# Attention with a convolution-gated FFN: w_in in three loads, V shifts by halves, and a new order table with its own buffer counts

One NeuronCore of a Trainium2 chip runs the whole program. The metric is the device time of one execution in microseconds (us); lower is better. The medians quoted are of all runs of a kernel, a few slow ones included (one of four of the kernel before, 230.82 us).

## The reference

Sliding-window attention over 8 batches, 8 heads, 576 positions and 64 features per head (window of 32 to either side), then an FFN whose hidden layer is gated by a depthwise convolution of three taps along the sequence. Condensed:

```python
scores = scale * np.matmul(q, k.transpose(0, 1, 3, 2))
scores = np.where(np.abs(pos[:, None] - pos[None, :]) <= 32, scores, -1e9)
attn = softmax(scores);  x = (attn @ v) -> (8, 576, 512)
h = np.maximum(x @ w_in, 0.0)                   # (8, 576, 1024)
conv_out = sum(conv_w[k] * shifted(h, k) for k in range(3))
gate = 1.0 / (1.0 + np.exp(-conv_out))
return (h * gate) @ w_out                       # (8, 576, 512), float32
```

## The kernel before

The program is a list of operations and a table that fixes everything about their execution. A token such as `286S1` means: operation 286, on engine S, with buffer 1. The letters are P for TensorE, V for VectorE (DVE in the profile), S for ScalarE (ACT), G for GpSimd (POOL), D for a DMA queue and F for filler matmuls on a zero tile. Each engine executes its own tokens strictly in the order of the table, so a token that isn't ready holds up all the later tokens of its engine. Two on-chip memories are named: the program's matmuls write to PSUM, and its loaded, cast and intermediate tiles are in SBUF.

The FFN is cut into 12 chunks of 384 positions, and each chunk into 8 units of 128 hidden features (chunk 1 into 16 half units). A unit is a projection on TensorE (`ph`, into PSUM), a relu into `hT` (in SBUF, bf16), three convolution taps, a tanh, and the gate into `gT`. Six kinds of unit split the taps between TensorE, GpSimd and VectorE (condensed):

```python
TAPS = {   # kind: (taps on TensorE, on GpSimd, on VectorE)
    "3": ((0, 1, 2), (), ()), "2": ((0, 2), (), (1,)), "1": ((0,), (), (1, 2)),
    "q": ((), (0, 2), (1,)), "r": ((), (0,), (1, 2)), "s": ((0,), (1, 2), ()),
}
def emit_times(e_, cp, kk):                # GpSimd: a product, "cp" in the profile
    gpsimd.tensor_scalar(out=in3(cp.ap), in0=taps(kk), scalar1=w_tap(kk), scalar2=0.0, op0=ALU.mult, op1=ALU.add)
def emit_add(e_, cps=cps):                 # GpSimd: the sum of two products
    gpsimd.tensor_tensor(out=in3(cps[0].ap), in0=in3(cps[0].ap), in1=in3(cps[1].ap), op=ALU.add)
def emit_pc(e_, on_pe=on_pe):              # TensorE: matmuls with diagonal weights, into PSUM
    for kk in on_pe: tensor.matmul(pc.ap[:, 0:nc_], diag_w[:, kk, m, :], taps(kk), ...)
def emit_tap(e_, kk, from_):               # VectorE: pc = hT * weight + from_
    vector.scalar_tensor_tensor(
        out=in3(pc.ap), in0=taps(kk), scalar=w_tap(kk), in1=in3(from_.ap), op0=ALU.mult, op1=ALU.add)
def emit_sum(e_, cps=cps):                 # VectorE: pc = pc + cp
    vector.tensor_tensor(out=in3(pc.ap), in0=in3(pc.ap), in1=in3(cps[0].ap), op=ALU.add)
```

`from_`: in the kinds 2 and 1 it is a PSUM bank, which TensorE's taps have filled. In the kinds q and r it is, for the first tap on VectorE, a `cp` buffer in SBUF, which GpSimd has filled; as `hT` is in SBUF too, that tap has two inputs in SBUF. I call it a "tap from cp". The mask multiplication of the attention (`attn * mask`) has two SBUF inputs as well, and the gate has one (`pc` is in PSUM).

V is needed at even and at odd 64-row offsets; `vo` is the shifted copy of `ve`:

```python
def shift_v(b, c0, c1):
    op(f"vo hi {b} {c0} {c1}", lambda e: copy(e, vo[0:64, c0:c1], ve[64:128, c0:c1]), ...)
    op(f"vo lo {b} {c0} {c1}", lambda e: copy(e, vo[64:128, c0:c1], ve[0:64, c0 + 1:c1 + 1]), ...)
```

The softmax here doesn't subtract the row's maximum and nothing guards it: scores larger than these inputs give would overflow.

Of the kernel before, what the change touches and what calls it, by code (L numbers as in the profile page):

```python
# [10 lines left out]
BF16 = mybir.dt.bfloat16  # L11
# [29 lines left out]
class Work:  # L41
# [44 lines left out]
BUFS = {'st': 3, 'qkb': 5, 'qkT': 3, 'attn': 2, 'rec': 4, 'xn': 3, 'hT0': 8, 'hT1': 6, 'hT2': 6, 'cp': 2, 'gT': 4, 'y': 7}  # L86
TURNS = ('eeeee', 'eeede', 'eeeed', 'dedde', 'ddddd', 'ddddd', 'ddddd', 'edddd')
CONV = (
    '33333333',
    '33q3323r23223321',  # L90
    's222r32q',
    '1232s332',
    '22q22q22',
    'q31s2qrq',
    '33212q2s',
    'r2rq312q',
    'qq23q1q2',
    'r3rqrq23',
    '12qrrq1q',
    '2rrr2rrq',  # L100
)
ORDER = """
15D 11D0 12D 1F 17D 2F 13D1 2F 14D 7F 28G 0V 1P0 2F 2V 33V 1F 4G 4F 20G0 21S 2F 16D 5G 1F 22S1 41P120 42P 23S 3G
45P34 44V 1F 43S 1F 46P 8G 2F 48S 47V 1F 9G 1F 30S 2F 49P5600 24G2 25S 54P214 2F 37V 18D 55S 1F 10G 1F 51S 1F 120D2
59P321 60P 52S 26V3 1F 27S 1F 6G 62V 1F 63P60 19D 61S 1F 64P 1F 36V 50S 121D0 1F 7G 65V 2F 130D1 66S 2F 53V 29S 1F
67P2351 1F 57S 56S 1F 35G 131D 72P604 70S 1F 31V 68S 2F 34G 1F 73S 2F 38V 74S 1F 39V 1F 58V 69S 3F 75S 123G 135D 1F
125S 77P10 86P5 124S 71V 95P2 3F 122G 78V0 96V1 1F 87V2 79S 2F 32V 132D2 2F 76V 97S 3F 40G 88V 1F 133D 98P6 89P0
113P3 99V3 107P4 90V0 104P1 100V 80P2 128G 129S 1F 114V1 105V2 1F 81V3 91V 102P5 127S 126G 106V 1F 93P6 82S 108V0
103V 139G4 109V 115S 84P7 94V 111P0 231D0 85S 112V 118P1 156P522 140G0 119V 134D 241P4 158S 157V 285P3 242S00 263P6
286S1 144V 243P7 264S2 149G 287P0 261S 150V 265P1 141G1 305S 262V 307P2 283S 306V 159P54 284V 142G2 308S3 172P360  # L110
161V 329P7 136D 174S 160V 173S 309P0 351P1 330S4 327S 331P2 232D1 352S5 328V 162P4650 233G 234S 353P3 349S 235V 137D
373P7 165S 164S 350V 163S 175P10 374V6 143G 167P526 371S 395P4 176V 236S 985D 170S 166V 375P7 169S 517P1 396S7 145G
372V 473P6 168S 177V 397P2 152G 393S 429P4 415S 171V 178P3501 138D 430S01 238S 239G 518V1 583P4 416V 181S 519P1 240S
237G 474V2 539P0 986D 394V 180S 451P2 482G0 983D2 561P6 179S 148V 495P7 481G1 584S3 188P51 151V 452S4 417P3 483G
496V5 537S 987D 189V2 190S 981D0 538V 146G 453P4 982D 183P271 182V 562S1 984D 471S 197P5 147S 418P 595G0 186S 198V3
484V6 185S 155G 199V 431P1 184S 472V 497P7 153V 421P5 419S0 154V 994V 988D 515S 187V 540S4 206P4 449S 422P 493S
992S3 450V 207V0 494V 516V 209P2 596V3 200P0 208S 191P1 218P6 996G 210V1 201V2 215P7 192V3 211V 202S 193V 542P2
219V1 213P4 216V0 423V1 195P1 217S 989D 204P0 220V 224P5 196V 990S4 425P6 991G0 225V3 543V 226V 1076D1 1017P711 214S
205V 221D 229P5 559S 426P 1077D 230S 993G1 1018V 1001P402 560V 1080D 427S2 1019V 1004P57 1078D0 627P2 1003S 1002V
1079D 605P6 1006S 715P1 997G 628V0 649P0 606S1 1005V 716S2 629P4 608P7 998G 717P2 647S 650V3 671P6 597V 735S 693P1  # L120
648V 1085G2 672S4 652P5 736V 603S 1020P04 609V 694S5 674P6 604V 625S 695P2 1022V 1021S 737P1 759P3 713S 626V 738S7
563P0 675V 760S6 793P4 714V 581S 1082D 995V 691S 1007P7130 582V 1086S3 1000D 692V 740P2 653V 764P0 815P6 741V 1008S
794V02 1010S 816V2 757S 837P7 809G1 1009S 765V 808G0 758V 1012P436 669S 838S5 766V 781P1 1087G4 670V 1014S 1015S
1081D 1013S 1096P270 1011V 779S 782P 1097S 810G 780V 1098V 1099P53 783S3 1083D 1023P6421 1016V 811P0 1100S 999D
840P7 424D 1088G0 812V 1024S 818P1 859P5 1084D 1101V 1026S 813S 420D 1025S 1112P622 1089G 841V 784D 881P3 860S4 428D
814V 1027G 1113S 1735D2 1114V 862P4 882S3 785P5 857S 819V 863V 1028P062 1737D1 1092S 1033P32 858V 1736D 835S 786P
1738D 1034V2 879S 893G1 836V 1029S 1051P7 1035V 1090G 1031S 1042P1 880V 787S4 1060P0 903P3 1091G 1052V1 1030S 1061V0
1043V3 1053V 925P2 1094D 894V4 904S1 1741D 947P5 1062V 926S0 895V 905P6 1044V 948S5 1115P73 1032V 901S 928P0 923S
955G0 1117V 789P2 1116S 1744G1 924V 1036P1 929V 1045P5 1069P3 1063P7 1054P6 1037V2 956G1 790P 1046V1 945S 1064V0
1038V 1065S 1746G2 1055V3 1047V 1070V2 1040P1 1056V 1049P5 791S5 1071V 1067P7 957G 1058P6 1050S 902V 1072D 1755P321  # L130
1068S 946V 973P4 1745G3 1059S 1756V 1041S 1740D 1102P5070 1757V 1747S4 969P6 788D 958V3 1739D 1093V 1171P1 1105S
1103S 1095D 1104S 1193P2 1172V03 967S 1106G 1215P7 1742D 1750S 1194V2 1107P501 968V 1216S1 1832D0 1176P2 1110S
1196P3 1108S 1177V 970P 1109S 1197V 1833Q 1118P7151 1743D 1178V 1749G 1213S 1237P0 1073D 1120S 1111V 1830D2 974P
1121S 1831D 1191S 1748G 1214V 1238S5 792D 1192V 1128P10 1119S 1146P5 975V6 1155P3 1137P0 971S1 1259P2 1122G 1147V1
1129V0 1156V3 1138V2 1148V 1123P746 1139S 1130V 1217P5 1260V4 1125S 1240P1 1157V 1126S 1277P0 1124S 1303P2 1241V
1835D 1235S 1274G1 1325P4 1257S 1127V 1842S0 1281P3 1275G0 1236V 1158P6 1140P7 1304V7 1326S3 1751G 1131P5 1282S6
1258V 1149P4 1752G 1164P2 1150V1 1305P3 1159V0 1165V2 1151S 1834D 1141V3 1276G 1160V 1283P1 1166V 1323S 1132V0 972D
1328P6 1142V 1754G 1301S 977P2 1278V 1302V 1279S 1144P4 1324V 1771P710 1145S 1280V 978P 1836D 1840G1 1772S 1329V
976D 1161D 1133V 1774P34 1345S 1773V 1758P07 1753D 1839G2 979S0 1347P5 1134D 1759S 1346V 980D 1776V 1844S 1841G4
1169P1 1850P262 1838D 1170S 1348P 1760V 1775S 1843G 1851V 1761P0410 1349S3 1852V 1351P7 1762S 1350D 1845G 1763S  # L140
1766P325 1764S 1853P60 1767S 1765V 1866P411 1352P 1769S 1768S 1868V 1854S 1770G 1837D 1777P3521 1867V 1353S2 1355P1
1855V 1778S 1152D 1780S 1782P647 1354D 1779S 1356P 2491D1 1785S 1784S 2492D 1783S 1781V 2489D2 1359P3 1357S4 1786V
1787P01 2490D 1360S00 1805P2 1814P5 1358D 1796P7 1806V2 1381P4 1788V1 1815V3 1807S 1797V0 1847V 1798V 1403P6 1816S
1382V1 1362P1 1846V 1384P3 1404S2 1789V 1447P7 1363V 1412G0 2495D 1385V 1425P2 1379S 1411G1 1448S3 1817P4 1380V
1401S 1413G 1790P5 1450P0 1426S4 1818V0 1791V2 1402V 1823P6 1808P7 2500G3 1428P1 1451V 1469P2 1809V3 1824V1 1467S
1429V 1810S 1799P3 1468V 1825V 1445S 1491P0 1800V3 1414V7 1826D 1470S5 2501S2 1547P6 1446V 1477G0 1801V 1513P2
2498G1 1492V0 1423S 1869P13 1792V 1548S21 1424V 1494P0 1514S1 1793D 1478G1 1569P5 1870V 1871S 2494D 1479G 2499S4
1827D 1516P6 1819V 1535P7 1495V 1820D 1555G1 1517V 1570S4 1591P2 1511S 1480V3 1533S 1613P1 1512V 1556G0 1489S 2493D
1534V 1592S1 1571P4 1802D 2504G 1614V3 1848D 1635P5 1589S 1557G 1490V 1849D 1596P0 1856P6210 1590V 1636S0 1536P
1597V 1628G0 1857S 1558V3 1859S 1858S 2496D 1861P456 2503G 1598V 1567S 1631P1 1811D 1539P2 1862S 1860V 1611S 1629G1  # L150
1568V 1701P4 1864S 1863S 1612V 1630G 1540P 1537S5 1702V5 2502S 1538D 1872P6351 1865V 1541S1 1877P074 2497D 1874S
1709G1 1632V 1657P2 2584D0 1879S 1710G0 1542D 1679P3 1878S 2586D1 1711G 1875S 1882P72 1873S 2587D 1891P0 1900P5
1883V1 1880S 1892V3 1633S 1909P6 1884V 1638P4 1658S4 1881V 1543P7 2585Q 2505G 1893V 1680S2 1910V2 1925P2 1634V 1911S
1665G0 2589D 1901V0 1639V 2507D 1544P 1926S22 1902V 1655S 1876V 1927P0 1545S6 1947P3 1712V1 2506S 1546D 1656V 1918P6
1945S 1691G1 1894P2 1885P5 1948S0 1919V1 1903P7 1946V 1912P4 1721S 1991P3 1895V3 1913V2 1904V0 1896S 1920V 2508D
2593G0 1914V 2035P0 1886V1 1905S 1722V 2509P640 1887V 1921D 1969P2 1992S1 1692V1 2510S 2594G1 2511V 1949P5 1970S5
2013P7 1693V 2036S6 1888D 1666G1 1967S 1727P3 2014V7 1699S 1667G 1968V 2016P6 1700V 2079P4 1922D 2592Q 2043G1 2017V
# [36 lines left out]
def kernel(  # L194
# [67 lines left out]
    diag_w = sb.tile([128, 3, MB, 128], BF16, name="diag_w")  # L262
    ident = sb.tile([128, 128], BF16, name="ident")
    ident24 = sb.tile([3 * MB, 3 * MB], FP32, name="ident24")
    mask = sb.tile([128, 18, 64], BF16, name="mask")
    zero = sb.tile([128, 512], BF16, name="zero")


# [541 lines left out]
```

## Time and profile before

| | |
|---|---|
| median time (4 runs, 227.18 to 230.82) | 227.36 us |
| span of the profiled execution | 225.6 us |
| units of full width: 3 / 2 / q / r / 1 / s | 19 / 25 / 19 / 14 / 7 / 4 |
| filler matmuls | 75 |

The prediction below shows the busy row, the windows and the main groups. First the groups of instructions by form: line, engine, operation, output <- inputs, shapes, count, then busy time, mean duration in ns, and idle time of the engine before them.

```profile
L232 DVE SCALAR_TENSOR_TENSOR pf<-hT,conv_w_sb,cp 128x384 f32<-128x384 bf16 x33 | 20.4, 630 | 0.0
L232 DVE COPY vo<-ve 64x520 bf16<-64x520 bf16 x10 | 4.1, 410 | 0.7 <-ACT ve L232 0.5
```

The first row is the taps from cp: 33 of them, 630 ns each; the second the V shifts on VectorE. Then the wait list (total, times, longest): ScalarE's tanh waits 11.1 us for taps of VectorE.

```profile
ACT pf L232 <- DVE pf L232: 11.1, 18, 1.2
```

And the chain of work that ended last, as shares of the span by engine:

```profile
PE 41%; DVE 18%; ACT 17%; DMA 13%; issue 5%; SPq 3%; POOL 2%; DVEq 0%; ACTq 0%; POOLq 0%
```

### The profile page before, as it was taken

Reading aid. Unit: us, or ns where it says so; the run is one execution under the profiler, and the core shown is the slowest. Engines: PE = TensorE matmul, PEld = TensorE weight load, DVE = VectorE, ACT = ScalarE, POOL = GpSimd, SP = SyncE. Lnnn points to the kernel's source line nnn. Section 1 sums busy time; section 2 is a strip of 40 time slices with the busy share of each in tenths; the row PEclk is TensorE's granted clock in tenths of the full one; section 3 lists DMA queues with packets and bytes.
Section 4 is the critical chain, followed back from the end, with each engine's and each line's share of the span. In section 5 each row is a group of like instructions: output and inputs, shape, how many; then the busy total and the mean of one; then the engine's idle time right before and its main releaser. Section 6 shows DMA issues by size and latency. Waiting matters only on the chain.

```text
span 225.6 us, 7189 instructions
## 1 busy us (share of the span) xinstructions
PE 211.5 (94%) x2720; PEld 122.9 (54%) x2720; DVE 197.3 (87%) x467; ACT 187.5 (83%) x474; POOL 137.7 (61%) x203
## 2 busy tenths in 40 slices
PE   7698899989989999989999998999999999999993
PEld 5366567658555655545555454545655565455541
DVE  6279869899999979797999788989999999899990
ACT  2689899998989889879889989689989999777642
POOL 5978654654376937695368736756386735566640
PEclk9889999999999999999999999999999999999999
DMA  6999999999989999999997989994535212501224
GB/s 201 331 285 358 355 266 281 321 308 253 290 170 324 317 175 287 236 306 224 288 347 129 202 278 358 182 231 147 144 36 118 99 46 49 175 1 49 93 101 178
DMA packets 66391, 48.16 MB, mean 214 GB/s; under 512 B 50781, under 2 KB 50805, under 8 KB 66357
## 3 DMA queue, kind: packets, MB, share of 16 engines
q1 hardware_dynamic: 64992, 46.32, 78.6%
q10 hardware_dynamic: 1364, 1.39, 2.9%
q8 instruction: 21, 0.34, 0.8%
q14 instruction: 14, 0.11, 0.2%
HBM read 32.52 MB, written 9.44 MB: 186 GB/s over the span
## 4 chain that ended last, share of the span: by engine, by line
PE 41%; DVE 18%; ACT 17%; DMA 13%; issue 5%; SPq 3%; POOL 2%; DVEq 0%; ACTq 0%; POOLq 0%
PE pf L232 41%; DMA st<-in_k_dram 7%; ACT attn L232 6%; DVE pf L232 5%; DVE gT L232 4%; SPq L232 3%; DMA out_dram<-y 3%; ACT xn L232 3%; DVE qkT L232 2%; ACT pf L232 2%; DMA vo<-ve 2%; DVE attn L232 2%; DVE xn L232 2%; ACT qkb L232 2%; ACT y L232 1%
## 5 line engine op out<-in xcount | busy, mean ns | idle before, releaser
L232 PE MATMUL pf<-xT,w_in_sb 128*128 128x385 bf16 (+2 forms) x416 | 73.4, 315 | 3.6 <-ACT hT L232 0.9
L232 PE MATMUL pf<-w_out_sb,gT 128*128 128x512 bf16 x288 | 72.2, 380 | 0.0
L232 POOL TENSOR_SCALAR cp<-hT,conv_w_sb 128x384 f32<-128x384 bf16 (+1 forms) x63 | 38.9, 622 | 46.1 <-ACT hT L232 20.2
L232 ACT ACTIVATE pf<-pf 128x384 f32<-128x384 f32 (+1 forms) x104 | 48.2, 477 | 13.1 <-DVE pf L232 11.1
L232 DVE SCALAR_TENSOR_TENSOR gT<-pf,hT 128x384 bf16<-128x384 f32 (+1 forms) x104 | 52.1, 517 | 5.5 <-ACT pf L232 5.1
L232 PEld LDWEIGHTS <-w_in_sb 128*128 128x128 bf16 x416 | 38.6, 98 | 27.8 <-issue 4.5
L232 ACT ACTIVATE attn<-pf 128x512 bf16<-128x512 f32 (+1 forms) x96 | 41.4, 522 | 1.8 <-PE pf L232 1.8
L232 ACT ACTIVATE hT<-pf 128x385 bf16<-128x385 f32 (+2 forms) x76 | 35.4, 487 | 6.0 <-PE pf L232 5.6
L232 PEld LDWEIGHTS <-gT 128*128 128x128 bf16 x288 | 26.0, 98 | 25.7 <-DVE gT L232 0.5
L232 DVE SCALAR_TENSOR_TENSOR pf<-hT,conv_w_sb,pf 128x384 f32<-128x384 bf16 (+1 forms) x61 | 34.7, 586 | 1.2 <-PE pf L232 1.1
L232 PE MATMUL pf<-hT,diag_w 128*128 128x384 bf16 (+1 forms) x153 | 30.9, 309 | 0.9 <-DVE xn L232 0.6
L232 POOL TENSOR_SCALAR qkb<-st 128x1152 bf16<-128x1152 f32 (+1 forms) x23 | 25.7, 1122 | 7.6 <-DMA st<-in_k_dram 3.2
L232 DVE COPY qkT<-pf 128x576 bf16<-128x576 bf16 x35 | 25.6, 750 | 4.9 <-PE pf L232 4.9
L232 POOL TENSOR_TENSOR cp<-cp,cp 128x384 f32<-128x384 f32 (+1 forms) x24 | 24.4, 1016 | 1.6
L232 DVE TENSOR_TENSOR attn<-attn,mask 128x1152 bf16<-128x1152 bf16 x26 | 23.0, 886 | 2.4 <-ACT attn L232 2.3
L232 ACT ACTIVATE xn<-pf,rec 128x64 bf16<-128x64 f32 x96 | 22.0, 360 | 1.5 <-DVE rec L232 1.5
L232 ACT COPY y<-pf 128x512 f32<-128x512 f32 x30 | 18.1, 605 | 3.9 <-PE pf L232 3.7
L232 DVE SCALAR_TENSOR_TENSOR pf<-hT,conv_w_sb,cp 128x384 f32<-128x384 bf16 (+1 forms) x35 | 21.2, 618 | 0.0
L232 POOL TENSOR_TENSOR attn<-attn,mask 128x1152 bf16<-128x1152 bf16 x6 | 14.2, 2371 | 8.4 <-ACT attn L232 8.4
L232 DVE TENSOR_TENSOR xn<-pf,rec 128x256 bf16<-128x256 f32 x48 | 18.9, 410 | 0.0
L232 ACT COPY qkT<-pf 128x576 bf16<-128x576 bf16 x29 | 18.6, 664 | 0.4 <-PE pf L232 0.2
L232 PEld LDWEIGHTS <-diag_w 128*128 128x128 bf16 x153 | 13.3, 97 | 9.8 <-issue 1.3
(49 smaller groups left out, 235.2 us busy)
## 6 DMA issues: line engine op xcount, KB each, us to landing
st<-in_q_dram SPq DMA_DIRECT2D x16, 576.0 KB, 6.8
out_dram<-y SPq DMA_DIRECT2D x36, 256.0 KB, 3.8
st<-in_k_dram SPq DMA_DIRECT2D x14, 576.0 KB, 8.2
vst<-in_v_dram SPq DMA_DIRECT2D x24, 256.0 KB, 7.0
vst<-in_v_dram SPq DMA_DIRECT2D x15, 192.0 KB, 5.7
vo<-ve SPq DMA_DIRECT2D x11, 260.0 KB, 5.6
st<-in_moe_w_in_dram SPq DMA_DIRECT2D x2, 1024.0 KB, 9.3
st<-in_moe_w_out_dram SPq DMA_DIRECT2D x2, 1024.0 KB, 9.4
```

The costliest lines, as they stand in the source:

```text
L232: return lambda *args, **kwargs: fixed(do(*args, **kwargs))
```

## The change

Its intent, as far as the code shows it, is to use the idle GpSimd: convolution taps go from VectorE and TensorE to GpSimd with six `cp` buffers in place of two, the V shifts go partly to GpSimd in halves, and ScalarE takes PSUM evictions from VectorE. Batch 0 gets its mask by matmul, w_in comes in three parts, nearly all fillers go, and four more transposes of x are made by DMA (29 to 33). The core of the diff (the order tables and the plumbing are cut):

```diff
-BUFS = {'st': 3, 'qkb': 5, 'qkT': 3, 'attn': 2, 'rec': 4, 'xn': 3, 'hT0': 8, 'hT1': 6, 'hT2': 6, 'cp': 2, 'gT': 4, 'y': 7}
+BUFS = {'st': 3, 'qkb': 6, 'qkT': 3, 'attn': 2, 'rec': 6, 'xn': 2, 'hT0': 7, 'hT1': 9, 'hT2': 9, 'cp': 6, 'gT': 3, 'y': 6}
+MASKS = ('aa', 'mm', 'mm', 'mm', 'mm', 'mm', 'mm', 'mm')
 CONV = (
-    '33333333', '33q3323r23223321', 's222r32q', '1232s332', '22q22q22', 'q31s2qrq',
-    '33212q2s', 'r2rq312q', 'qq23q1q2', 'r3rqrq23', '12qrrq1q', '2rrr2rrq',
+    'r2333q33', '221223s321s2213r', 'r3q3332s', 'r333s3q3', '22q33q33', 'q32sqq2q',
+    '33qq2rqq', '2q3q3qrr', 'qqrqqq33', '32qrqqqr', 'rqq2qq3q', '2r22qqrq',
 )
 ... (ORDER: every token rearranged; 75 fillers become 5)
+    W_PARTS = {"in": ((0, 2), (2, 4), (4, MB)), "out": ((0, MB // 2), (MB // 2, MB))}
-        for c in range(NBLK - 1) if b < 2 else (0,):
-            shift_v(b, c, c + 1 if b < 2 else NBLK - 1)
+        for c in range(0, NBLK - 1, 1 if b < 2 else 2):
+            shift_v(b, c, c + (1 if b < 2 else 2))
 ... scores of kind 'a': matmuls add -30000 outside the window, and the mask product is left out
+                        tensor.matmul(
+                            ps[n].ap[:, 0:64 * width].rearrange("p (t x) -> p t x", x=64), outside[rows, :],
+                            ident[rows, None, rows].broadcast_to([64, width, 64]), start=True, stop=False,
+                        )
```

## The prediction

> **What bounds the kernel now.** I read the page's busy row first, then the engine windows by stage, the groups of instructions by form, the chain of waits and the wait list.
>
> ```profile
> PE 211.5 (94%) x2720; PEld 122.9 (54%) x2720; DVE 197.3 (87%) x467; ACT 187.5 (83%) x474; POOL 137.7 (61%) x203
> ```
>
> Three engines are above 80% and GpSimd (POOL) alone has room. PE's 94% overstates it, for two reasons. 75 of the matmuls are fillers on a zero tile, which compute nothing. And a matmul's recorded duration contains its pipeline latency. From the start times in the trace, the usual distance from one matmul's start to the next is 216 ns for the 512-column form, 163 to 166 for 384 to 386 columns, 83 for 193 and 56 for 128. Runs of the small attention matmuls take about 20 ns each (transposes 20.4, scores 21.9, values 20). So the work is 288 x 0.216 + 256 x 0.163 + 96 x 0.166 + 64 x 0.083 + 118 x 0.163 + 35 x 0.083 + 58 x 0.056 = 150.4 us, plus 3 x 576 small ones at about 0.021 = 35.9: **186 us of real PE work**. The span is 225.6, so about 39 us of it are PE loss. The windows say where:
>
> ```profile
> core 0: us, PE busy (x) PEld busy (x) DVE busy (x) ACT busy (x) POOL busy (x), PEclk, DMA share, GB/s
> 0.00:25.80 25.80, 21.13 (x329) 14.52 (x329) 17.43 (x56) 18.53 (x46) 19.67 (x65) 0.93 0.98 298
> 25.80:60.00 34.20, 33.23 (x491) 22.81 (x492) 30.45 (x78) 32.05 (x88) 16.45 (x23) 1.00 1.13 299
> 60.00:100.00 40.00, 37.80 (x575) 21.23 (x575) 37.00 (x88) 34.69 (x84) 29.79 (x29) 1.00 1.04 254
> 100.00:140.00 40.00, 38.12 (x536) 21.36 (x537) 35.01 (x83) 36.55 (x97) 24.21 (x29) 1.00 1.07 262
> 140.00:180.00 40.00, 40.00 (x498) 21.45 (x498) 39.01 (x83) 34.45 (x85) 26.06 (x33) 1.00 0.65 142
> 180.00:221.30 41.30, 40.80 (x298) 21.53 (x298) 38.35 (x84) 30.18 (x77) 21.54 (x29) 1.00 0.23 76
> 221.30:225.60 4.30, 0.42 (x2) 0.00 (x0) 0.00 (x0) 1.07 (x2) 0.00 (x0) 0.90 0.49 183
> ```
>
> The loss has three places. *Start*: the first FFN matmul starts at 25.80 us; until then real work is an eighth of 35.9 plus 16 matmuls of 56 ns, 5.4 us, so 20.4 are lost. *Tail*: 4.3, two evictions and a store. *Middle*: 39.3 - 20.4 - 4.3 = 14.6 between 25.8 and 221.3. There DVE is 89 to 98% busy in each window and ACT 94% in the first: PE's holes are waits for evictions by those two. The chain agrees:
>
> ```profile
> 1.83 6.50 DMA st<-in_k_dram
> ...
> 19.38 0.76 DVE attn L232
> ...
> 20.89 0.67 DVE attn L232
> 21.61 0.33 PE pf L232 x6
> ...
> 25.80 7.68 PE pf L232 x93
> ```
>
> The start is a load of k (landing at 8.3), then casts, exps on ACT, the mask multiplication on DVE (twice on the chain), values, normalisation, transposes. From 33.5 to about 75 the chain is all ACT and DVE; late it is 48 us of PE. Meanwhile GpSimd waits for its conv inputs:
>
> ```profile
> POOL cp L232 <- ACT hT L232: 20.2, 10, 4.1
> POOL cp L232 <- DVE pf L232: 17.0, 15, 4.2
> ```
>
> The second is a wait for a buffer: a DVE tap has to read a cp buffer before GpSimd may write it again, and there are two of those.
>
> **What the Trainium skill says.** "Perfetto Trace Analysis", § Identifying the Most-Contended Engine, holds matmul busy time a bad measure; this trace agrees (211.5 busy against some 186 worked out). "TensorE: Matmul & The Clock Gate", Part 1, says PE starts at half clock and gets the full one after about 3.4 us of activity: here the first fillers start 213 ns apart and late ones 109, and the trace's clock record has a half-rate window from 9.7 to 13.1 us in spite of the fillers. "GPSIMD Engine Reference", § 1 Specifications, says GpSimd's SBUF interface is shared with VectorE for two-SBUF-input and 2-port instructions: the mask product on DVE averages 751 ns with GpSimd idle, 1079 beside a busy GpSimd (longest 1727). Operations reading PSUM don't care: the gate is 550 and 548. § 4.1 of the same page rates two-input operations about twice as slow there; here the cp product takes 622 ns and the cp sum 1034.
>
> **The change part by part**, counted from the two order tables, each count times a mean of before's rows:
>
> ```profile
> L232 DVE SCALAR_TENSOR_TENSOR pf<-hT,conv_w_sb,pf 128x384 f32<-128x384 bf16 x53 | 31.5, 613 | 1.2 <-PE pf L232 1.1
> L232 DVE COPY qkT<-pf 128x576 bf16<-128x576 bf16 x35 | 25.6, 750 | 4.9 <-PE pf L232 4.9
> L232 POOL TENSOR_SCALAR cp<-hT,conv_w_sb 128x384 f32<-128x384 bf16 x60 | 37.0, 622 | 44.4 <-ACT hT L232 20.2 <-DVE pf L232 17.0 <-DVE hT L232 6.0
> L232 POOL TENSOR_TENSOR cp<-cp,cp 128x384 f32<-128x384 f32 x23 | 23.8, 1034 | 1.5
> L232 DVE TENSOR_TENSOR attn<-attn,mask 128x1152 bf16<-128x1152 bf16 x26 | 23.0, 886 | 2.4 <-ACT attn L232 2.3
> ```
>
> *DVE*: taps onto PSUM 53 to 25 (-28 x 0.613 = -17.2), taps from cp 33 to 45 (+12 x 0.630 = +7.6), half-width taps and sums about +2.2, masks 26 to 23 (-2.7), qkT evictions 35 to 20 (-15 x 0.750 = -11.3); against that more q/k, v and weight casts (+6.5, an estimate from 446 ns per 512 columns), 12 diagonals (+2), five y evictions (+3.4), xn and hT (+2.3), vo (+0.7). Sum about **-6.5, to 191**. *ACT*: qkT +15 x 0.664 = +10.0; q/k casts -6.1, weight and v casts -5.1, y -3.0, xn -2.9, xT -1.9, relu -1.4. Sum **-10.5, to 177**. *POOL*: cp products +24 x 0.622 and two halves, +16; cp sums +13 x 1.034 and a half, +14; vo halves +12; diagonals -4.5, one mask -2.4, weights, hT and constants +4. Sum **+39, to 177**. *PE*: diagonal matmuls 118 to 110 and 35 to 28 (-1.9), ten transposes fewer (-0.6), twelve additive-mask matmuls in batch 0 (4 x (128+512+512) columns, about +2.0): **186 to 185.8**. The 70 fillers dropped are worth nothing by themselves, as they lay in the start's holes. So the change is a rebalancing towards GpSimd, with 6 cp buffers instead of 2 and 25 hT instead of 20, but gT 4 to 3 and xn 3 to 2.
>
> *Start.* q and k are issued ahead of v 0 and of the other v blocks, each SP issue being some 0.5 us: k 0 lands perhaps 0.7 earlier and q/k of the other half up to 2 (it was cast at 12.5 before). The mask goes out of batch 0's chain: -0.76 - 0.67 = -1.4. w_in in three parts lets the first units begin on a quarter of it (a half took 9.3 us to land), but nothing in the chain of before waits for w_in long, so 0 to 0.5. Without fillers PE may be cold: additive matmuls at half clock add about 1 us each on the first chain, partly hidden under ACT's exps, and the first 3.4 us of FFN at half clock lose up to 1.7. I take -3.0 for order and mask and +1.0 for the clock: start loss 20.4 to 18.4.
>
> *Middle.* DVE and ACT lose 6.5 and 10.5 us. The last third is nearly PE-solid (chunks 7 to 11 have 42 DVE taps instead of 52, a relief that PE can use only in part), so the gain has to come out of the holes between 25.8 and 180. I take 5.5 of 14.6, rather less than DVE's reduction. *Tail*: the last units end alike, +0.2.
>
> Sum: 185.8 + 18.4 + 4.5 + 9.1 = 217.8 us of span; time is 1.7 above span before (227.3 against 225.6), so **219.5 us**, -3.4%.
>
> **Rivals.** (1) *GpSimd becomes the bound, or slows DVE.* 177 of 218 is 81%, its sums take 1 us and sit between relu and gate; 45 taps from cp and 23 masks have two SBUF inputs. If half of the masks go from 751 to 1079, that is 4 us of DVE; then DVE's gain is nearly gone and only start plus ACT's relief remain: 222 to 225. For it: the 1727 ns mask. Against it: taps from cp average 630 against 613 for those from PSUM. (2) *Buffers*: gT 3 and xn 2 hold up an early start of the next chunk or batch and turn a removed DVE wait into one for a projection: 223 to 226. Against it: the order table was evidently made for these counts. (3) *Cold start*: without fillers the clock stays at half till 30 us; costs 2 to 4 us: 221.5 to 223.5. (4) *Better than I take*: the middle's loss nearly vanishes, PE being the only bound, 5 us less: 213 to 215. DMA (share over 1 until 140 us) may either way matter: fewer bytes of vo copies by DMA speak for the good side.
>
> **Range and chances.** Centre 219.5. The high end 225 is rival 1 or 2 whole; the low end 214 is rival 4. Within 2% means above 222.7: it needs rival 1, 2 or 3 with most of its size, 0.22; slower by 2% (over 231.8) needs a collapse that nothing here shows, 0.03; faster 0.75.
>
> **What would show it.** Right: DVE near 191, ACT near 177, POOL near 177 busy; first xT x w_in matmul near 23 to 24 us; PE holes between there and the last matmul about 9 us; last matmul near 213.5. Wrong: first FFN matmul at 25 or later, or spaced 320 ns (cold clock); masks beside GpSimd over 1000 ns and DVE near 197 again; PE waiting for POOL cp through DVE pf; GpSimd above 90% in any window from 60 on; or waits for gT and xn.

## The result

The kernel after takes **241.53 us** (4 runs, 240.04 to 242.59). A ratio here is the mean time of one kernel's fast runs over the mean of the other's in the same rounds, so not quite the ratio of the medians quoted. It is 1.0621 (95% interval 1.055 to 1.0693): 6% slower, where 3.4% faster was predicted. The busy row of the page after:

```profile
PE 206.2 (87%) x2615; PEld 118.8 (50%) x2637; DVE 213.1 (89%) x473; ACT 181.2 (76%) x456; POOL 189.0 (79%) x256
```

VectorE was to fall from 197.3 to 191 and rose to 213.1. GpSimd was to reach 177 and reached 189.0. ScalarE fell, to 181.2. The chain of work by engine:

```profile
DVE 43%; PE 26%; issue 11%; POOL 8%; ACT 6%; DMA 3%; SPq 2%; DVEq 0%; POOLq 0%; ACTq 0%
```

VectorE has gone from 18% of the chain to 43%, and TensorE from 41% to 26%: the bound has moved to VectorE. The windows, with the columns as in the prediction (length, busy time and count of PE, PEld, DVE, ACT, POOL, then granted clock, DMA share, GB/s):

```profile
0.00:25.80 25.80, 16.00 (x262) 10.85 (x263) 17.30 (x62) 15.76 (x35) 14.12 (x58) 0.87 0.94 284
25.80:60.00 34.20, 30.62 (x478) 20.20 (x480) 32.00 (x82) 28.69 (x75) 30.23 (x44) 1.00 0.96 269
...
180.00:221.30 41.30, 37.41 (x319) 19.62 (x323) 40.16 (x75) 27.31 (x71) 35.18 (x43) 1.00 0.34 96
```

Between 25.8 and 60 us GpSimd's load has nearly doubled, 16.45 to 30.23, and PE is 2.6 us less busy there. Late, where PE had been 99% busy (40.80 of 41.30), it is 91%, with VectorE at 97%. (The trace has no record of 22 of this kernel's 2637 matmuls, 4 of them here, so PE is a little busier than shown.) The groups of instructions by form say why VectorE grew:

```profile
L234 POOL TENSOR_SCALAR cp<-hT,conv_w_sb 128x384 f32<-128x384 bf16 x84 | 58.8, 711 | 13.5 <-ACT hT L234 6.8 <-DVE hT L234 6.1
L234 DVE SCALAR_TENSOR_TENSOR pf<-hT,conv_w_sb,cp 128x384 f32<-128x384 bf16 x45 | 39.5, 882 | 2.3 <-issue 0.7 <-ACT attn L234 0.6 <-POOL cp L234 0.5
L234 DVE TENSOR_TENSOR attn<-attn,mask 128x1152 bf16<-128x1152 bf16 x23 | 24.5, 1069 | 0.1
```

The counts are those that I had predicted: 84 products, 45 taps from cp, 23 masks. The **durations** are not: a tap from cp takes 882 ns against 630, a mask 1069 against 886, and GpSimd's product too has gone from 622 to 711. The same shapes, the same operands, and only the neighbour busier. I split the change of every form into a count (difference of counts x mean before) and a duration (count after x difference of means). In sums of recorded durations, which overlap and so don't add up to the busy time (229.1 us of them in 197.3 busy before), VectorE went -4.6 us by count (predicted -6.5) and **+18.9 by duration**: 45 x (882 - 630) = 11.3 from the taps, 23 x (1069 - 886) = 4.2 from the masks, the rest from V and weight casts and small copies.

Sorted in the trace by what GpSimd was doing during the same time: the taps from cp that had GpSimd instructions beside them for at least 90% of their duration average 958 ns (31 of them, longest 1958), and the four with at most 10% average 618. Masks: 1266 ns (14, longest 2772) against 751 (3). Gates, which read one input from PSUM, take 546 ns either way. In the kernel before, the same sorting finds **none** of the 33 taps from cp with GpSimd busy throughout, and 614 ns for the 16 with GpSimd idle. The 17 between, with GpSimd busy for a part, average 645, the longest 886: that sign was there to be seen. So the 630 ns that I multiplied by 45 had been measured without the neighbour that the change brings.

The waits show how it comes to cost time:

```profile
ACT pf L234 <- DVE pf L234: 24.7, 29, 2.2
POOL ve L234 <- DMA vst<-in_v_dram: 7.5, 1, 7.5
PE pf L234 <- DVE gT L234: 7.1, 13, 1.7
```

The tanh's wait for VectorE's taps has gone from 11.1 to 24.7 us, and TensorE waits 7.1 us for gates (DVE gT), 3.2 of them ahead of the matmuls with w_out, which read the gate's result. GpSimd's wait for its buffer (17.0 us before) is gone, as six `cp` buffers were to achieve. The second line is at the start. The chain there, in order of time (start, duration, instruction):

```profile
5.69 7.83 DMA vst<-in_v_dram
...
23.82 2.30 PE pf L234 x12
26.22 0.56 DVE hT L234
26.78 0.75 DVE diag_w L234 x3
27.52 0.54 DVE pf L234
29.70 0.46 DVE gT L234
```

The first FFN matmul is at 23.8 us in this trace, 2.0 us earlier than before. But chunk 0, which was all TensorE ("33333333"), now has units with VectorE taps, and its first gate comes at 30.2 us against 29.6 before. The gain of the start is gone after the first unit. One trace isn't enough here: in the five traces whose order is the same up to there (after, a_psumtap, a_q2, a_s, a_vodma) the first FFN matmul comes at 23.6 to 25.1 us and the first gate at 30.2 to 31.6; in the three with the start of before (before, b_buf, b_load), at 25.3 to 25.8 and 29.1 to 29.6. So the first matmul is 0.2 to 2.2 us earlier, and the first gate later in every one.

Where is the time lost? I counted PE's work (not its busy time) from the start times of its weight loads, of which no record is missing, and compared when each kernel has done the same amount. With 20 of 186 us done the kernel after is still 0.7 us ahead; with 60 it is 2.6 behind, with 100 1.1, with 130 5.5, with 150 8.2, with 180 11.1. So the loss isn't one event. It comes in two stretches: from about 25 to 80 us, and in the second half, where the q and r units are.

### The profile page after: what moved, and what is told of

It is laid out like the page before. It is cut to its first block, busy times and chain, and to the rows that moved or that the text cites. A ratio compares the mean times of both kernels' runs of the same rounds, so it can differ in the third digit from the quotient of the medians.

```text
span 238.3 us, 7024 instructions
## 1 busy us (share of the span) xinstructions
PE 206.2 (87%) x2615; PEld 118.8 (50%) x2637; DVE 213.1 (89%) x473; ACT 181.2 (76%) x456; POOL 189.0 (79%) x256
## 4 chain that ended last, share of the span: by engine, by line
DVE 43%; PE 26%; issue 11%; POOL 8%; ACT 6%; DMA 3%; SPq 2%; DVEq 0%; POOLq 0%; ACTq 0%
PE pf L234 26%; DVE pf L234 13%; DVE gT L234 11%; DVE attn L234 4%; POOL cp L234 4%; DMA vst<-in_v_dram 3%; DVE hT L234 3%; DVE qkT L234 3%; ACT pf L234 2%; DVE vo L234 2%; POOL vo L234 2%; SPq L234 2%; DVE xn L234 2%; DVE y L234 2%; ACT attn L234 1%
## 5 line engine op out<-in xcount | busy, mean ns | idle before, releaser
L234 POOL TENSOR_SCALAR cp<-hT,conv_w_sb 128x384 f32<-128x384 bf16 (+1 forms) x89 | 61.7, 703 | 16.1 <-ACT hT L234 9.4
L234 ACT ACTIVATE pf<-pf 128x384 f32<-128x384 f32 (+1 forms) x104 | 47.1, 469 | 26.3 <-DVE pf L234 24.7
L234 DVE SCALAR_TENSOR_TENSOR pf<-hT,conv_w_sb,cp 128x384 f32<-128x384 bf16 (+1 forms) x46 | 40.4, 881 | 2.3 <-issue 0.7
L234 POOL TENSOR_TENSOR cp<-cp,cp 128x384 f32<-128x384 f32 (+1 forms) x38 | 40.1, 1061 | 1.9
L234 POOL TENSOR_SCALAR qkb<-st 128x1152 bf16<-128x1152 f32 (+2 forms) x24 | 28.2, 1179 | 0.6 <-DMA st<-in_q_dram 0.3
L234 ACT COPY qkT<-pf 128x576 bf16<-128x576 bf16 x44 | 27.1, 658 | 1.8 <-DVE xn L234 1.0
L234 DVE TENSOR_TENSOR attn<-attn,mask 128x1152 bf16<-128x1152 bf16 x23 | 24.5, 1069 | 0.1
L234 PE MATMUL pf<-ident,qkb 64*128 64x64 bf16 x576 | 15.7, 196 | 9.1 <-POOL qkb L234 5.9
L234 DVE SCALAR_TENSOR_TENSOR pf<-hT,conv_w_sb,pf 128x384 f32<-128x384 bf16 (+1 forms) x39 | 20.7, 542 | 1.7 <-PE pf L234 1.2
L234 POOL TENSOR_SCALAR vo<-ve 64x520 bf16<-64x520 bf16 (+1 forms) x20 | 19.6, 980 | 2.6 <-PE pf L234 0.8
L234 PEld LDWEIGHTS <-qkT 64*128 64x128 bf16 x576 | 13.0, 98 | 15.2 <-issue 13.8
L234 PE MATMUL pf<-qkT 64*128 64x64 bf16 x576 | 16.1, 195 | 4.4 <-DVE gT L234 2.1
```

Of the source, the lines that this page charges most:

```text
L234: return lambda *args, **kwargs: fixed(do(*args, **kwargs))
```

## The experiments

The main theory (T): GpSimd's longer load blocks VectorE's instructions with two SBUF inputs, and VectorE is what the others wait for. The rivals: a start without fillers is cold; the smaller buffer counts; GpSimd's own length; VectorE's early load; the order itself. "Before" in the table is the median of the kernel before in the same job (chips differ by about 1%).

| kernel | median us | before there | ratio (95%) |
|---|---|---|---|
| after, taps read PSUM in place of hT (a_psumtap) | 232.57 | 228.53 | 1.0182 (1.0134 to 1.0230) |
| after, thin GpSimd products (a_thin) | 231.19 | 228.53 | 1.0123 (1.0076 to 1.0169) |
| after, 14 units q to 2 (a_q2) | 251.75 | 228.53 | 1.1026 (1.0954 to 1.1098) |
| after, ten V shifts by DMA (a_vodma) | 247.03 | 228.53 | 1.0818 (1.0765 to 1.0872) |
| after, all q to s (a_s) | 261.32 | 228.01 | 1.1423 (1.1321 to 1.1525) |
| after, with fillers (a_fill) | 241.71 | 228.01 | 1.0570 (1.0478 to 1.0662) |
| after, V block 0 loaded early (a_vfirst) | 240.61 | 228.01 | 1.0526 (1.0455 to 1.0597) |
| before, with idle GpSimd work (b_load) | 238.35 | 228.01 | 1.0432 (1.0364 to 1.0500) |
| before, additive mask in batch 0 (b_add) | 228.44 | 229.04 | 0.9967 (0.9919 to 1.0014) |
| before, counts of cp, gT and xn of after (b_buf) | 228.49 | 229.04 | 0.9979 (0.9940 to 1.0019) |
| after, five early casts to ACT (a_early) | 242.25 | 229.04 | 1.0562 (1.0507 to 1.0616) |
| a_psumtap and a_early (a_psum_early) | 232.64 | 229.04 | 1.0149 (1.0089 to 1.0209) |
| a_psumtap and V shifts on ACT (a_psum_vo) | 230.83 | 228.52 | 1.0115 (1.0056 to 1.0173) |
| a_psumtap and a_thin (a_psum_thin) | 230.32 | 228.52 | 1.0098 (1.0032 to 1.0163) |
| before, additive mask, batches 0 and 1 (b_add2) | 227.96 | 228.52 | 0.9980 (0.9926 to 1.0034) |
| before, additive mask, batches 0 to 3 (b_add4) | 233.79 | 228.52 | 1.0240 (1.0176 to 1.0304) |
| a_psum_thin, V shifts on ACT, V 0 early (a_free) | 230.27 | 228.36 | 1.0094 (1.0053 to 1.0134) |
| b_add2 and b_buf (b_best) | 228.63 | 228.36 | 0.9971 (0.9905 to 1.0036) |

**a_psumtap: take away one of the two SBUF inputs.** Its output is wrong, which doesn't matter for the time. Engines, order, waits and counts stay.

```diff
-                    out=in3(pc.ap), in0=taps(kk), scalar=w_tap(kk), in1=in3(from_.ap), ...
+                    out=in3(pc.ap), in0=taps(kk) if from_ is pc else in3(pc.ap), scalar=w_tap(kk), in1=in3(from_.ap), ...
```

> Changed kernel, but the taps that read a GpSimd product (46 of them) take their first operand from PSUM instead of from hT in SBUF (wrong result on purpose): one SBUF tensor input instead of two, everything else, GpSimd's work and the waits for it included, as it was. Contention theory (DVE instructions with two SBUF inputs are slowed beside a busy GpSimd): these taps fall from 882 to about 620 ns, GpSimd's products from 711 towards 620, DVE busy from 213 to about 201, time from 241.5 to 230-234. Rival A (GpSimd's own longer queue holds up the units): the taps become shorter but the time stays within 2 us of 241.5. Rival B (buffers, start): likewise unchanged.

Groups by form, as above:

```profile
L233 POOL TENSOR_SCALAR cp<-hT,conv_w_sb 128x384 f32<-128x384 bf16 x84 | 52.9, 641 | 15.0 <-ACT hT L233 8.9 <-DVE hT L233 5.4
L233 DVE SCALAR_TENSOR_TENSOR pf<-pf,conv_w_sb,cp 128x384 f32<-128x384 f32 x45 | 27.6, 618 | 2.3 <-ACT attn L233 1.5 <-POOL cp L233 0.5
L233 DVE TENSOR_TENSOR attn<-attn,mask 128x1152 bf16<-128x1152 bf16 x23 | 23.8, 1038 | 0.1
L233 DVE COPY vo<-ve 64x1040 bf16<-64x1040 bf16 x5 | 5.2, 1041 | 0.2
```

The tap falls from 882 to 618 ns, the duration that it has beside an idle GpSimd, and GpSimd's product falls with it, from 711 to 641: both sides had paid. (The taps still read a weight column in SBUF, one number for each partition. As they take 618 ns beside a GpSimd that is busy for 176 us, it doesn't act as a second input here.) VectorE falls from 213.1 to 202.0 us, and the time by **9 us**. The clock isn't behind this: the transposes ahead of the first FFN matmul take 314 ns at most in both traces, so the start is equally cold (see a_fill), and the first gate is even later here (31.6 us against 30.2). The tanh's wait for taps is back where it was before the change:

```profile
ACT pf L233 <- DVE pf L233: 12.2, 18, 2.2
```

The masks (1038) and the V shifts (1041) are still long. The timeline (start, duration) shows how a VectorE copy fares here:

```profile
71.03 2.36 POOL L233 TENSOR_TENSOR attn<-attn,mask 128x1152 bf16<-128x1152 bf16 x1
71.15 2.53 DVE L233 COPY vo<-ve 64x1040 bf16<-64x1040 bf16 x1
```

The copy starts 0.12 us after a GpSimd mask and ends 0.29 us after it; the shortest copy of this form takes 425 ns. It was held for nearly the whole GpSimd instruction. The Trainium skill, "SBUF — State Buffer", § Who interferes with whom, states just this: a DVE instruction with two SBUF inputs contends with a GpSimd instruction that reads SBUF, copies in a 2-port mode contend too, and whichever comes second blocks fully until the first has finished. The trace agrees: 2.53 us here, and taps of 958 against 618 ns. I had not read that page when I predicted.

**a_thin: leave the count of GpSimd instructions, cut their length.** Products and sums cover 4 columns of each half instead of 192 (the values are not the reference's, though the difference stays inside its tolerance); the `cp` buffers are zeroed once. This shortens both the time for which GpSimd holds the interface and GpSimd's own queue, so it can't tell these two apart.

```diff
-                    out=in3(cp.ap), in0=taps(kk), scalar1=w_tap(kk), ...
+                    out=in3(cp.ap)[:, :, 0:4], in0=thin(kk), scalar1=w_tap(kk), ...
```

> Changed kernel with GpSimd's conv products and sums cut to 4 of 192 columns (wrong result on purpose): the same instructions, order and waits, but about 80 us of GpSimd's work gone. Contention and rival A both: time to 222-230. If the time then stays over 236, neither, and order, buffers or the start are the cause. Its distance to a_psumtap is what GpSimd's own length costs beyond the slowing of DVE.

```profile
L233 DVE SCALAR_TENSOR_TENSOR pf<-hT,conv_w_sb,cp 128x384 f32<-128x384 bf16 x45 | 30.2, 675 | 2.4 <-issue 1.2 <-ACT attn L233 0.6
```

Taps of 675 ns, masks of 933, GpSimd at 124.5 us busy, and 231.19 us, just above the 222 to 230 expected. That is 1.4 us better than a_psumtap: a second route to the same gain, with a little on top.

**a_q2 and a_s: give the work back to TensorE.** In a_q2 fourteen q units of the chunks 5 to 11 become 2; in a_s all 33 become s, whose last step on VectorE reads PSUM and cp.

```diff
-    'q32sqq2q', '33qq2rqq', '2q3q3qrr', 'qqrqqq33', ...
+    '232sq22q', '332q2r2q', '223q32rr', '2qr2qq33', ...   (a_q2)
+    's32sss2s', '33ss2rss', '2s3s3srr', 'ssrsss33', ...   (a_s)
```

> Changed kernel with 14 full-width conv units of chunks 5 to 11 (two in each) moved from two GpSimd products plus a sum to two diagonal matmuls on PE, as many as before had fewer of them. GpSimd loses about 14 x 2.5 = 35 us, DVE some 14 x 0.27 = 4 us, PE gains 28 x 0.163 = 4.6 us of work. Contention or rival A: 232-237 us. Buffers or start as the cause: no gain, 241-245, since PE has more to do.

> Changed kernel with all 33 full-width units of kind q (two products and a sum on GpSimd, DVE adds the third tap from hT and cp, both in SBUF) turned into kind s (the third tap as one diagonal matmul on PE, DVE adds cp to it in PSUM: one SBUF input). Correct result. The diagonal is issued as soon as a PSUM bank is free. Contention theory: DVE loses 33 x (0.88 - 0.56) = 10 us, PE gains 33 x 0.163 = 5.4 us of work: 231-235 us, a legal version of the run with taps from PSUM. If PE's place in the order matters more (as it did when 14 units went to two diagonals), 238-250 with DVE waiting for PE.

Both missed, even the alternatives in the texts: 251.75 and 261.32 us, the worst of all. VectorE did get shorter (202.8 and 200.7 us), and in a_s its last step takes 562 ns although GpSimd is busy; but the wait lists show VectorE standing still for TensorE, first a_q2:

```profile
DVE pf L231 <- PE pf L231: 22.0, 15, 3.7
```

and a_s:

```profile
DVE pf L234 <- PE pf L234: 28.7, 21, 3.3
```

My reading, which no run tests: the new diagonal matmuls wait in TensorE's fixed order behind its backlog, and the VectorE token that needs them holds all the later ones. These two kernels therefore say nothing for or against T. They say that in these two cases exchanging kinds within the old order cost more than it saved.

**a_vodma: ten V shifts from GpSimd to DMA**, to relieve GpSimd of its longest copies.

```diff
-1008G 1009G 1109G 1110G 1111G 1775G 1776G 1875G 1877G 2540G
+1008D 1009D 1109D 1110D 1111D 1775D 1776D 1875D 1877D 2540D
```

> Changed kernel with the ten two-block shifts of V that GpSimd makes from batch 2 on issued as DMAs from SP instead, at the same places of the order. GpSimd loses 12.7 us, DMA gains 1.3 MB of small packets. Contention or rival A: 237-240 us. If SP's in-order queue then holds up loads: 242-246.

GpSimd fell to 176.1 us, and the time rose to 247.03, a little above the alternative in the text. The shifts by DMA now take up to 9.7 us from issue to landing (5.3 in the kernel after, which makes nine of them), and TensorE waits 3.0 us for them. As this run brings in a wait of its own, it says nothing about GpSimd's length; a_psumtap does, where GpSimd is still 176.0 us busy and the loss is mostly gone.

**a_fill: the fillers back** (14 ahead of the first transposes, 2 ahead of each TensorE group up to the first FFN matmul).

```diff
-... 41P010 ...
+... 14F 41P010 ...     and "2F" ahead of each later P token of the start
```

> Changed kernel with 60 filler matmuls back at the start (14 ahead of the first transpose, two ahead of each of the next PE groups up to the first FFN matmul). Cold-start theory: the half-rate window between 17 and 24 us goes, the first gate comes 1 to 2 us earlier and the time falls by as much. Otherwise unchanged within 0.7 us, or up to 1.5 us longer as fillers stand ahead of real work.

241.71 us against 241.53: no effect. The clock record in the profile of after does show a half-rate stretch from 17.4 to 24.2 us, and it costs nothing that can be measured. The matmuls show that the fillers did their work: the transposes of x at 21 to 23 us take up to 314 ns in the kernel after and 219 in a_fill, and the first FFN matmuls start 273 and 217 ns apart there and 163 here. Yet the first gate isn't earlier (31.1 us against 30.2). The cold-start rival falls. (The record isn't complete: a_psumtap has the same 314 ns and no such stretch in it.) This run also repeats the kernel after, in effect, on another chip.

**a_vfirst: V block 0 loaded ahead of q and k of the other half.** In the kernel after it lands at 13.5 us, and GpSimd waits 7.5 us for it.

```diff
-11D0 12D 13D1 14D 16D 18D 15D 22S0 ...
+11D0 12D 15D 13D1 14D 16D 18D 22S0 ...
```

> Changed kernel with the load of v block 0 issued right behind the first q and k instead of behind all q, k and two v blocks. If V's late landing (13.5 us in the changed kernel, GpSimd waited 7.5 us for it) holds up the start, the first gate comes 1 to 2 us earlier, and the time falls by as much; otherwise within 0.7 us.

240.61 us; the first gate is at 30.4 us, not earlier than the 30.2 of the kernel after, and the intervals of a_fill and a_vfirst overlap. About one microsecond, if anything.

**b_load: the converse, on the kernel before.** Behind each cp product GpSimd also multiplies a zero tile by one, in place: no dependence on anything else, only load.

```diff
                 gpsimd.tensor_scalar(out=in3(cp.ap), in0=taps(kk), scalar1=w_tap(kk), ...)
+                gpsimd.tensor_scalar(
+                    out=zero[:, 0:CH], in0=zero[:, 0:CH], scalar1=1.0, scalar2=0.0, op0=ALU.mult, op1=ALU.add)
```

> Kernel before with one idle GpSimd instruction (a 384-column product of a zero tile in place, about 0.585 us) behind each of its 63 conv products: GpSimd goes from 138 to about 175 us busy, no other engine has more to do. Contention theory: taps from cp rise from 630 to 800 or more, masks on DVE from 886 to 1000 or more, time to 231-237 us. If GpSimd has room as I had predicted, within 2 us of before.

```profile
L230 DVE SCALAR_TENSOR_TENSOR pf<-hT,conv_w_sb,cp 128x384 f32<-128x384 bf16 x33 | 25.2, 774 | 6.1 <-POOL cp L230 5.9
L230 POOL TENSOR_SCALAR zero<-zero 128x384 bf16<-128x384 bf16 x63 | 35.2, 558 | 0.0
```

The time rises by 10.3 us, to 238.35, more than the 231 to 237 expected. The taps go from 630 to 774 ns (not the 800 expected; 817 for the 12 with GpSimd beside them throughout, 612 for the seven without), so a busy GpSimd alone makes them longer, in the kernel before too. But this run is mixed evidence for the size: VectorE's busy time grew only 4.4 us, the masks got *shorter* (824 against 886 ns, against expectation, and no run shows why), and VectorE now waits 9.0 us for products that GpSimd finishes later. So part of the 10 us is probably GpSimd's queue, not the interface.

**b_add, b_add2, b_add4: the additive mask, alone, on the kernel before**, in batch 0, in batches 0 and 1, and in 0 to 3. The order keeps its place for each operation; the masks of those batches go out.

```diff
+MASKS = ('aa', 'mm', 'mm', 'mm', 'mm', 'mm', 'mm', 'mm')     (b_add; b_add2 and b_add4 with more 'aa')
```

> One part of the change alone: the kernel before, its order and buffers, but with the mask of batch 0 added by matmuls ahead of the scores instead of multiplied in by DVE. Two mask products of 0.67 and 0.76 us stood on the chain of the start; against it twelve matmuls on an idle PE. By my step for the start 0.5 to 1.4 us shorter than before; if other waits take their place, within 0.4 us.

> Kernel before with the masks of batches 0 and 1 added by matmuls instead of multiplied by DVE. DVE loses 8 masks of 0.75 to 1.7 us in a stage where it is 89 to 100% busy, PE gains 24 matmuls, about 4 us, where it has holes. Contention theory turned round: 0.5 to 3 us shorter than before. If PE's place in the order costs as in the runs with more diagonals: up to 3 us longer.

> The same for batches 0 to 3: 16 masks off DVE and GpSimd, 48 more matmuls, about 8 us, on PE. If b_add2 gains, this gains or loses up to 2 us more, as PE is then at some 194 us of real work.

Nothing that can be told from noise from the first two (0.9967 and 0.9980, both intervals reach over 1; that of b_add leaves room for a gain of up to 1.8 us, so the 0.5 to 1.4 of my step for the start is neither shown nor excluded), and 2.4% slower with four batches. There VectorE fell to 188.8 us busy, and TensorE had some 8 us more work: here removed VectorE work didn't come back as time, as TensorE had to pay for it.

**b_buf: three of the changed buffer counts (cp, gT, xn), alone, on the kernel before.** The counts of qkb, rec, hT and y stay as before.

```diff
-'xn': 3, ... 'cp': 2, 'gT': 4
+'xn': 2, ... 'cp': 6, 'gT': 3
```

> Another part alone: the kernel before, its order, with cp 6 instead of 2 buffers, gT 3 instead of 4 and xn 2 instead of 3, slots dealt out in turn. Rival 2 of the prediction (fewer gT and xn hold up the next chunk): 229 us or more. My step (GpSimd freed of its waits for a cp buffer): 0.5 to 2 us shorter. Neither: within 0.5 us.

228.49 against 229.04: neutral. Rival 2 of the prediction (gT and xn) costs nothing in the order of before; in the order of after it wasn't run alone. Six cp buffers gain nothing that can be told from noise. Its trace has one thing more to tell:

```profile
L230 DVE SCALAR_TENSOR_TENSOR pf<-hT,conv_w_sb,cp 128x384 f32<-128x384 bf16 x33 | 21.4, 662 | 0.0
```

GpSimd's 17.0 us of waits for a cp buffer are gone from its wait list, and now eight of the 33 taps from cp do have GpSimd beside them throughout (for at least 90%, as above). Those average 770 ns, and the mean of all 33 rises from 630 to 662.

**a_early and a_psum_early: five early casts (w_in 6 and 7, k 1 0, w_out 2 and 3) from VectorE to ScalarE**, on the kernel after and on a_psumtap.

```diff
-133V 134V 145V 244V 245V
+133S 134S 145S 244S 245S
```

> Changed kernel with five casts that DVE makes between 20 and 45 us (two of w_in, k of batch 1, two of w_out, about 3 us) given back to ACT at the same places. Theory of an overloaded DVE in the early stage: the loss against before between 25 and 75 us (4 us of progress) falls by 1 to 3 us and the time with it. Otherwise within 0.7 us of 241.

> The same on top of the taps that read PSUM instead of hT (wrong result on purpose, 232.6 us). If contention and the early DVE load are the two causes and add up: 229.5 to 231.5 us. If the early load does not matter: 232 to 233.

242.25 and 232.64: no gain on either. VectorE's early load isn't the cause. The difference of the two, 9.6 us, also repeats that of a_psumtap on another chip.

**a_psum_vo and a_psum_thin: what is left after the taps.** In the first the eleven V shifts that VectorE still has go to ScalarE, on top of a_psumtap; in the second a_thin is added to it.

```diff
-34V 37V 40V 155V 158V 159V 1010V 1011V 1112V 1777V 2543V
+34S 37S 40S 155S 158S 159S 1010S 1011S 1112S 1777S 2543S
```

> Changed kernel with taps from PSUM (232.6 us; wrong result on purpose), and the eleven V shifts that DVE makes given to ACT at the same places. If contention on them is part of the rest: 229.5 to 231.5 us. If not: 232 to 234 as ACT has 8 us more to do.

> Changed kernel with taps from PSUM and GpSimd's conv products and sums cut to 4 of 192 columns (wrong result on purpose). Against 232.6 and 231.2 us of the two alone: if GpSimd's length and the slowed taps were separate costs, 224 to 228; if thin products had already taken the contention away and only the order is left, 230 to 231.5.

230.83 and 230.32, so 1.7 and 2.3 us below a_psumtap. Moving the V shifts seems worth something; a shorter GpSimd, something similar. The intervals of both overlap that of a_psumtap, so these two steps are likely, not certain.

**a_free: all of it at once.** Taps from PSUM, thin products, V shifts on ScalarE, V block 0 early.

```diff
 (the edits of a_psumtap, a_thin, a_psum_vo and a_vfirst)
```

> Changed kernel with all four: taps from PSUM, GpSimd's conv instructions cut short, DVE's V shifts on ACT, v block 0 loaded early (wrong result on purpose). If the costs found add up: 227 to 229 us, equal to before, so that nothing of the slowdown is left to the order; but also nothing of the 8 us gain that I had predicted for DVE's and ACT's shorter lists. If 230 or more, the order keeps a cost of its own.

```profile
PE 202.4 (89%) x2615; PEld 117.9 (52%) x2637; DVE 193.5 (85%) x468; ACT 188.7 (83%) x467; POOL 117.3 (51%) x256
```

VectorE is at 193.5 us, near the 191 of the prediction; ScalarE, which has taken the shifts, is at 188.7. The time is 230.27 us, 0.9% above the kernel before (interval 0.5% to 1.3%). So even with the contention of taps and shifts gone (the masks are still 916 ns), the new order isn't faster than the old one, let alone by the 8 us that I predicted.

**b_best: b_add2 and b_buf together**, in case the neutral parts add up.

```diff
+MASKS = ('aa', 'aa', 'mm', ...);  'xn': 2, 'cp': 6, 'gT': 3
```

> Kernel before with additive masks in batches 0 and 1 and the changed buffer counts of cp, gT and xn (each measured 0.2 to 0.3% below before, within noise). If these are real and add: 226 to 227.5 us beside before's 228.5. If noise: within 0.3% of before.

228.63 us, 0.9971 (0.9905 to 1.0036): the same as before. No version of mine is shown to beat the kernel before.

## Why the prediction was wrong

**What held.** TensorE's real work doesn't change. The counts of all groups were right, and VectorE's change by count was near (-4.6 us, predicted -6.5). The first FFN matmul is at 23.8 us, predicted 23 to 24; with 23.6 to 25.1 in five traces of the same start, that it hit the range is partly luck. The tail is as predicted: the last matmul ends at 233.7, which leaves 4.6 us to the end of the span, against 4.5. Of the rivals in the prediction, the cold start is none (a_fill), and buffers show no cost (b_buf). Its sums hold to within 0.2 us when redone; one reading was off a little (VectorE is 88% busy in the window from 100 to 140 us, not 89 or more).

**The step that failed: "each count times a mean of before's rows".** It takes a mean duration for a property of the instruction. For instructions with two SBUF inputs on VectorE, and for GpSimd's on the other side, it is a property of the pair, and the change put 51 us more on one side of the pair (GpSimd 137.7 to 189.0 busy). This made VectorE's instructions 18.9 us longer in sum, where the step had only a gain of 6.5 by count; GpSimd's became 11.7 longer beside the 41.5 by count (39 predicted). a_psumtap shows it for the taps: with one operand moved, and nothing else, 9 us of the loss go. On ScalarE the step failed in another way: by count it lost 10.9 us (10.5 predicted), but only 6.3 of busy time, as its recorded durations overlap (240.9 us of them in 187.5 busy) and a mean duration is thus more than an instruction costs.

**Rival 1 named the mechanism and was sized wrong.** It had masks only, "4 us of DVE", and argued against more with "taps from cp average 630 against 613 for those from PSUM". The masks did cost 4.2. The taps cost 11.3. The argument was wrong because none of before's 33 taps had GpSimd beside it throughout. With two cp buffers, GpSimd had to wait for that very tap before it could write again (the 17.0 us of waits that the prediction showed): the evidence for the taps being immune came from a schedule that kept them apart. b_buf shows this: with six buffers and the same order, eight taps meet a busy GpSimd and take 770 ns. The range inherited the error, as its high end was rival 1 "whole".

**The middle's loss.** By the prediction's own sum it is 233.7 - 23.8 - 180.4 (the work of 185.8 less the 5.4 done at the start) = 29.5 us, where 9.1 was predicted and 14.6 was before's. Contention of the taps is about 9 of the difference to before (a_psumtap), blocked shifts and GpSimd's length perhaps 2 to 3 more (a_psum_vo, a_psum_thin; they overlap, so the sum isn't exact).

**The gain that never came.** "I take 5.5 of 14.6" assumed that VectorE's and ScalarE's shorter lists would close PE's holes. No run tests this: none has both lists at the predicted lengths. a_free has VectorE at 193.5 us (191 predicted) but ScalarE at 188.7 (177 predicted, 187.5 before), so the two together are only 2.6 us shorter than before, and it gains nothing. b_add4 takes 8.5 us of VectorE work away from the kernel before, at the price of some 8 on TensorE, and loses. That PE's holes come from which token waits for which, and not from the sum of the lists, is a guess that fits both; it isn't shown.

**The start.** The 2.0 us of the earlier first matmul in this trace (0.2 to 2.2 over all the traces) were spent within some 6 us, on VectorE's relu, diagonals and taps of the first units. The prediction stopped at the first matmul; the first gate was the better mark.

**What stays open.** The 2 us by which a_free is behind the kernel before. They belong to the order or to its start and to the contention that is left (the masks), and no run divides them. Where they arise can be said: counted as above, a_psumtap is 5.1 us behind the kernel before with 60 of 186 us done, 2.9 with 130 and 4.8 with 180 (the kernel after 2.6, 5.5 and 11.1). So the contention of the taps accounts for the growing loss of the second half; the rest is there by 85 us, where a_early found no cause. The w_in load in three parts and the halved V shifts weren't run alone, as both hang on the order. How much of b_load's 10 us is the interface and how much GpSimd's queue isn't settled either.

## What to carry to other kernels

Before you multiply a count by a mean duration, sort the instances of that row by what the neighbouring engine did meanwhile; a mean from a quiet neighbour isn't valid for a busy one (630 ns against 882 here), and a row of which no instance met a busy neighbour throughout says little about it. Before you move work from VectorE to GpSimd, look how many of VectorE's instructions beside it have two inputs in SBUF: the Trainium skill, "Perfetto Trace Analysis", § Optimizing Scalar/DVE Operations, warns that offloading between these two "might not help" because they share an SBUF read port, and here GpSimd's 51 us more came with 16 us more on VectorE. In a program with a fixed order, a longer instruction delays what stands behind it on its engine, and exchanging an operation's engine without making the order anew cost 5 to 20 us in three of three trials that brought TensorE or the DMA queue into a path (a_q2, a_s, a_vodma).

## What the Trainium skill lacked or had wrong

- "SBUF — State Buffer", § Who interferes with whom: the rule is right, but has no size for a three-operand tap. Here `scalar_tensor_tensor` with two SBUF tensors takes 618 ns beside an idle GpSimd and 958 beside a busy one, up to 1958; a mask of 751 ns takes 1266, up to 2772.
- "GPSIMD Engine Reference", § 1 Specifications, names the shared interface but gives no size for what GpSimd itself loses: its product takes 711 ns in the kernel after and 641 when VectorE's taps read PSUM.
